# Out units that change PSUM banks behind a pair of scores instead of at a TensorE drain

## Chip, cores and metric

The kernel runs on one NeuronCore of a Trainium2 chip. The metric is the device time of one execution in microseconds (us); lower is better. TensorE (PE) has a loader for weights (PEld) beside its matmuls; VectorE is DVE, ScalarE is ACT, GpSimd is POOL, SyncE is SP.

## What is computed

With x of 2048 tokens by 576 channels in fp32:

```
g = sigmoid((x * gate_w).sum(-1))
q, k, v = split(x @ wqkv), 32 heads of 18
a = concat(softmax(q k^T / sqrt(18)) v) @ wo
h = gelu(layernorm(x) @ w1 + b1)            # 576 -> 4608
b = h @ w2 + b2                             # 4608 -> 576
out = g * a + (1 - g) * b
```

## The kernel before

Matmul operands that need it are split into a high and a low part, and a product is the sum of three matmuls (high x high, high x low, low x high). A first stage projects q, k and v, normalizes x and writes the pieces to scratch in device memory. Then one long loop does attention and the MLP together, and the output projection follows at its end.

**The loop** runs over 32 attention units (two heads and half of the queries each) and 16 steps of 128 keys in each, 512 steps. A step does two sets. A set is `s2`, a pair of score matmuls of the second pass (L247; two row groups of TensorE, one head each) whose two results ScalarE turns into exponentials (L250), and `next_round`, a pair of score matmuls of the first pass (L206) for a later unit whose row maxima VectorE takes (L208). The scores go round a ring of five PSUM banks, `score_bank`; a set uses four of them. On even steps the products of exponentials with V (`pv`, L265) stand behind the first set of the step.

**The MLP fills in.** `mlp` is a generator that issues one pair of matmuls at a time and says where a piece ends (`cut`). `fill` takes one piece (`atom`) behind a set: none behind the first set of an even step, where `pv` stands, one behind the second (`piece[0]` = 0), one behind each set of an odd step (`piece[0]` = 1 and 2). So four sets and three pieces make a round of two steps.

There are two kinds of MLP work. `h_pair` makes two chunks of 128 hidden channels for 512 tokens: 27 pairs of matmuls with 512 columns (L443) into two banks of the pool `ps_w`, then the gelu on ScalarE (L464, L496, L494) and GpSimd, handed out by `defer` (so many slots later) and `queue_end` (when the planner's clock `now` has passed the end that it reckons for GpSimd's queue). `out_pair`, an *out unit*, multiplies four chunks for 128 tokens with w2: 24 pairs of matmuls with 288 columns (L523), again into two banks of `ps_w`, which VectorE adds to the accumulator (L532). A group of four chunks takes one `h_pair`, then the four out units of the group before, then the other `h_pair`; there are 36 groups and 144 out units.

In an out unit, row group 0 holds one half of the hidden channels and row group 1 the other. In the first turn, 12 pairs, row group h adds into bank h; in the second turn, 12 pairs, into bank 1 - h. Two row groups may not write one bank at a time, so the first turn has to be through before the second begins. The kernel before has a drain on TensorE's queue at that place (L512).

The pieces of a unit that begins behind the second set of an even step are 7, 8 and 9 pairs (`ends = {7, 15}`), so the drain stands inside the middle piece, behind five of its eight pairs.

Of the kernel before, what the change touches and what calls it, by code (L numbers as in the profile page):

```python
# [8 lines left out]
F32 = mybir.dt.float32  # L9
F32R = mybir.dt.float32r  # L10
AF = mybir.ActivationFunctionType
# [16 lines left out]
G = 4  # L28
NFC = F // P
NG = NFC // G  # L30
ND = 288
# [26 lines left out]
def gated_mix_kernel(ctx: ExitStack, tc: tile.TileContext, x, wqkv, wo, w1, b1, w2, b2, gate_w, out):  # L58
    nc = tc.nc
# [3 lines left out]
    const = ctx.enter_context(tc.tile_pool(name="const", bufs=1))  # L63
# [14 lines left out]
    ident = const.tile([P, P], F32, name="ident")  # L78
# [19 lines left out]
    def psum(pool):  # L98
        return pool.tile([P, TB], F32, name="ps")
# [27 lines left out]
    def defer(n, fn):  # L127
        later.append((slot[0] + n, fn))
# [189 lines left out]
    def mlp():  # L318
# [65 lines left out]
        def ready(table, key):  # L384
            while key not in table:
                bg.pop(0)[1]()
            return table[key]
# [23 lines left out]
                          lambda c: load_w2(c + 2))  # L411

        open_pairs = [0]

        def cuts(n, pieces):

            return {(k * n + pieces - 1) // pieces for k in range(1, pieces)}
# [83 lines left out]
        def out_pair(i, t, acc):  # L501

            tb, g = seq[i]
            tok = slice(t * P, (t + 1) * P)
            cs = [slice(nn * ND, (nn + 1) * ND) for nn in range(2)]
            ps = [psum(ps_w) for _ in range(2)]
            ends = {7, 15} if piece[0] == 0 else cuts(24, (3, 2, 1)[piece[0]])
            k = 0
            for turn in range(2):
                if turn == 1:  # L510

                    nc.tensor.drain()  # L512
                for j in ORDER:
                    while (i, j) not in HT:
                        cut[0] = 3
                        yield 0
                    hh, hl = HT[i, j]
                    w_ = ready(W2, (i * (G // 2) + j // 2, j % 2))
                    for h_, p_ in ((hh, 0), (hh, 1), (hl, 0)):
                        for h in (0, 1) if turn == 0 else (1, 0):  # L520
                            r = slice(64 * h, 64 * h + 64)
                            nn = h ^ turn
                            nc.tensor.matmul(ps[nn][:, :ND], h_[r, tok], w_[p_][r, cs[nn]],  # L523
                                             start=(k == 0), stop=(k == 6 * G - 1))
                        k += 1
                        if k < 6 * G:
                            if k in ends:
                                cut[0] = 1
                            yield 131
            for nn in range(2):  # L530
                dst = acc[:, t, cs[nn]]
                nc.vector.scalar_tensor_tensor(dst, ps[nn][:, :ND], 0.5, b2b[:, cs[nn]] if g == 0 else dst,  # L532
                                               op0=ALU.mult, op1=ALU.add)
            if g == NG - 1:
                tt = tb * 4 + t
                nc.gpsimd.tensor_scalar(acc[:, t, :], acc[:, t, :], gate1[:, tt:tt + 1], 1.0, op0=ALU.mult, op1=ALU.mult)

                def store():
                    nc.sync.dma_start(b_scr[tt * P:(tt + 1) * P, :], acc[:, t, :])
                    kept[0] += 1  # L540
                defer(12 if tb < NB - 1 else 4, store)
            cut[0] = 2
            yield 131
# [7 lines left out]
        def outs(i, between=()):  # L551

            tb, g = seq[i]
            if g == 0:
                ACC[tb] = x_tile().rearrange("p (t d) -> p t d", t=4)[:, :, :D]
            for t in range(4):
                if t == 2:
                    yield from between
                yield from out_pair(i, t, ACC[tb])
            for j in range(G):  # L560
                HT.pop((i, j))
                W2.pop((i * (G // 2) + j // 2, j % 2))
# [22 lines left out]
        for i in range(n + 1):  # L585
# [10 lines left out]
            if i < n and not inside:  # L596
                yield from pair(q + 1, held)

    stream = [mlp()]
    spent = [0.0]  # L600
    cut = [0]
    piece = [0]
# [31 lines left out]
    with ExitStack() as a:  # L634
# [172 lines left out]
        for tb in range(NB):  # L807
            work = [(qk_group, (tb, mt)) for mt in (range(9) if tb < 2 else (4, 0, 1, 2, 3, 5, 6, 7, 8))] + [(v_group, (tb, t, n)) for t in range(4) for n in range(2)]
            for g, (fn, args) in enumerate(work):
# [22 lines left out]
                if tb == NB - 1:  # L832
# [16 lines left out]
                    if g == 7:  # L849
                        ps = psum(ps_s1)  # L850
# [283 lines left out]
```

## Time and profile before

| | us |
|---|---|
| median of 3 runs | 2382.97 (2378.87 to 2385.91) |
| the profiled execution | 2379.91 |
| its span, first to last instruction | 2378.1 |
| TensorE matmuls, busy | 2308.8 (97%) |
| VectorE, busy | 1655.4 (70%) |
| ScalarE, busy | 1425.9 (60%) |
| mean granted TensorE clock | 0.987 |

A line of the timeline gives start, length, engine (PEld is the weight load), source line, operation, what is written from what, shape, and how many instructions it merges; in square brackets the idle time of the engine ahead of it and what ended it. In a source line's answer, "issue" is idle time that ended without any other engine's release. Ends of matmuls are modelled, starts are recorded, so the distances below are taken between starts.

### The profile page before, as it was taken

What the parts mean: (1) busy time and instruction counts of PE and PEld (TensorE: products, weight loads), DVE (VectorE), ACT (ScalarE), POOL (GpSimd) and SP (SyncE); (2) the same over time, 40 slices, a digit from 0 to 9 for tenths busy, and PEclk for the clock granted to TensorE, in tenths of its full rate; (3) what the DMA queues carried; (4) which work ended last, traced back from release to release, by engine and by line L of the source; (5) the groups of instructions that cost most, each with busy time, mean ns of one, the idle gap of its engine ahead of it and who ended that gap; (6) DMA issues with size and microseconds to landing.
All of it is one profiled execution on the core that took longest, in us unless ns stands there. A gap on an engine that the chain in (4) does not pass through costs nothing.

```text
span 2378.1 us, 51603 instructions
## 1 busy us (share of the span) xinstructions
PE 2308.8 (97%) x20585; PEld 1571.9 (66%) x20585; DVE 1655.4 (70%) x2890; ACT 1425.9 (60%) x2628; POOL 968.3 (41%) x964
## 2 busy tenths in 40 slices
PE   8999899999999999999999999999999999999889
PEld 7876566666666666666666666666656666666558
DVE  5467577777776777777777777777767777777424
ACT  4222367777676666666666666666656666666552
POOL 3001366666664433333454444433343334444500
PEclk9999899999999999999999999999999999999899
DMA  7748744545455423342354424232545343331254
GB/s 229 243 166 235 211 146 137 166 129 151 134 185 163 156 94 116 104 140 97 98 153 161 130 85 131 94 116 94 142 137 166 112 119 114 92 115 66 96 181 157
DMA packets 164874, 330.31 MB, mean 139 GB/s; under 512 B 57898, under 2 KB 84558, under 8 KB 153906
## 3 DMA queue, kind: packets, MB, share of 16 engines
q1 hardware_dynamic: 163050, 323.78, 43.4%
q8 instruction: 162, 2.65, 0.5%
q10 hardware_dynamic: 1584, 3.24, 0.4%
q14 instruction: 78, 0.64, 0.1%
HBM read 234.16 MB, written 96.58 MB: 139 GB/s over the span
## 4 chain that ended last, share of the span: by engine, by line
PE 89%; DMA 5%; DVE 3%; SPq 1%; issue 1%; ACT 0%; POOL 0%; DVEq 0%; ACTq 0%
PE ps L523 20%; PE ps L265 19%; PE ps L443 18%; PE ps L247 12%; PE ps L206 11%; PE ps L755 4%; PE ps L1030 2%; PE ps L776 2%; DVE m L208 1%; DMA big<-y_scr 1%; DMA x<-in_B_w_dram 1%; DMA v_scr<-vt 0%; PE ps L682 0%; SPq L121 0%; SPq L372 0%
## 5 line engine op out<-in xcount | busy, mean ns | idle before, releaser
L208 DVE TENSOR_REDUCE m<-ps 128x1 f32<-128x512 f32 x2048 | 1316.7, 685 | 478.5 <-PE ps L206 460.1
L250 ACT ACTIVATE p<-ps 128x512 f32<-128x512 f32 x1368 | 742.9, 596 | 435.9 <-PE ps L247 425.6
L162 POOL TENSOR_SCALAR zz<-zz 128x512 f32<-128x512 f32 x288 | 179.4, 623 | 843.6 <-ACT zz L496 828.6
L443 PE MATMUL ps<-big,w 64*128 64x512 f32 x3888 | 513.9, 394 | 0.1
L523 PE MATMUL ps<-w,hh 64*128 64x288 f32 x4352 | 491.2, 300 | 19.3 <-DMA w<-w_scr 7.1
L250 ACT ACTIVATE ring<-ps 128x512 f32<-128x512 f32 x680 | 369.4, 596 | 213.3 <-PE ps L247 206.5
L206 PE MATMUL ps<-ka,qa 54*128 54x512 f32 x2048 | 457.0, 416 | 14.3 <-DVE m L208 7.9
L247 PE MATMUL ps<-qa,ka 56*128 56x512 f32 x2048 | 455.3, 425 | 10.9 <-ACT p L250 5.3
L523 PEld LDWEIGHTS ps<-w,hh 64*128 64x128 f32 x4352 | 383.6, 186 | 76.2 <-issue 45.2
L443 PEld LDWEIGHTS ps<-big,w 64*128 64x128 f32 x3888 | 380.1, 186 | 76.9 <-ACT z L464 0.4
L162 POOL TENSOR_TENSOR zz<-zz,z 128x512 f32<-128x512 f32 x288 | 372.5, 1294 | 24.0
L247 PEld LDWEIGHTS ps<-qa,ka 56*128 56x128 f32 x2048 | 205.5, 185 | 227.8 <-DVE m L208 176.6
L265 PE MATMUL ps<-p,vt 128*32 128x512 f32 x2736 | 348.7, 604 | 2.7 <-DMA vt<-v_scr 2.7
L523 PE MATMUL ps<-w,hl 64*128 64x288 f32 x2176 | 334.6, 292 | 0.0
L206 PEld LDWEIGHTS ps<-ka,qa 54*128 54x128 f32 x2048 | 213.5, 187 | 87.8 <-ACT p L250 24.1
L162 POOL TENSOR_TENSOR w<-x,w 128x576 fp32r<-128x576 f32 (+1 forms) x54 | 98.5, 1837 | 317.2 <-DMA y_scr<-hh 169.1
L523 PEld LDWEIGHTS ps<-w,hl 64*128 64x128 f32 x2176 | 218.5, 185 | 4.9
L162 POOL TENSOR_TENSOR hl<-zz,hh 128x512 fp32r<-128x512 f32 x136 | 176.6, 1299 | 11.3
L265 PE MATMUL ps<-ring,vt 128*32 128x512 f32 x1360 | 180.5, 603 | 0.0
L265 PEld LDWEIGHTS ps<-p,vt 128*32 128x32 f32 x2736 | 72.0, 109 | 164.1 <-issue 153.7
L532 DVE SCALAR_TENSOR_TENSOR x<-ps,x 128x288 f32<-128x288 f32 x256 | 104.1, 449 | 23.7 <-PE ps L523 23.7
L755 PE MATMUL ps<-big,wqk 128*128 128x512 f32 x432 | 111.7, 408 | 2.9 <-ACT wqk L676 2.3
(98 smaller groups left out, 1374.4 us busy)
## 6 DMA issues: line engine op xcount, KB each, us to landing
w<-w_scr SPq DMA_DIRECT2D x54, 1152.0 KB
w<-w_scr SPq DMA_DIRECT2D x108, 576.0 KB
x<-in_B_w_dram SPq DMA_DIRECT2D x72, 288.0 KB
w_scr<-w SPq DMA_DIRECT2D x18, 1152.0 KB
w_scr<-w SPq DMA_DIRECT2D x36, 576.0 KB
big<-y_scr SPq DMA_DIRECT2D x42, 384.0 KB
qa<-qk_scr SPq DMA_DIRECT2D x192, 72.0 KB
ka<-qk_scr SPq DMA_DIRECT2D x84, 144.0 KB
```

The lines of the kernel that those rows point to most:

```text
L162: fn(*args, **kw)
L206: nc.tensor.matmul(ps, qa[r0:r0 + 54, t * P:(t + 1) * P], ka[r0:r0 + 54, kb * TB:(kb + 1) * TB], start=True, stop=True)
L208: nc.vector.tensor_reduce(M4[u][:, h, t, kb:kb + 1], ps, axis=AX.X, op=ALU.max)
L247: nc.tensor.matmul(ps[h], ka[r0:r0 + 56, kc * P:(kc + 1) * P], qa[r0:r0 + 56, qb * TB:(qb + 1) * TB], start=True, stop=True)
L250: nc.scalar.activation(RING[n % 3][:, qb, h], ps[h], AF.Exp, scale=SCALE)
L265: nc.tensor.matmul(OB[u][r:r + 32, :], v[:, k, 19 * h:19 * h + 32], RING[c % 3][:, qb, h, :], start=(k == 0), stop=(k == NT - 1))
L443: nc.tensor.matmul(ps[h], wt[w_][r, c, :], Y[s_][r, c, :], start=(k == 0), stop=(k == 26))
L523: nc.tensor.matmul(ps[nn][:, :ND], h_[r, tok], w_[p_][r, cs[nn]], start=(k == 0), stop=(k == 6 * G - 1))
L532: nc.vector.scalar_tensor_tensor(dst, ps[nn][:, :ND], 0.5, b2b[:, cs[nn]] if g == 0 else dst, op0=ALU.mult, op1=ALU.add)
L755: nc.tensor.matmul(ps, w_[:, c, ms], big[:, s_, :], start=(k == 0), stop=False)
L776: nc.tensor.matmul(ps[:, :ND], big[:, s_, tok], w_[:, c, cs], start=(k == 0), stop=False)
L1030: nc.tensor.matmul(ps[:, :ND], OT[b][2][:, s_, tok], w_part(w_, c)[:, cs], start=(k == 0), stop=(k == 13))
```

## The change

The drain is taken out. The first turn's last two matmuls now release a tiny activation on ScalarE, which copies one element of the identity into a one-element tile (`token`), and the second turn's first two matmuls wait for that activation. The edge of the first piece moves to the change of banks, so that a set of scores stands between the two turns: a unit that begins behind the second set of an even step has pieces of 12, 6 and 6 pairs; one that begins in another place has two pieces of 12 (before, two of 12 or one of 24). ScalarE's queue has the token ahead of the exponentials of the set that follows. The reserve for GpSimd's DMA descriptors in SBUF is set to 1024 bytes.

```diff
         open_pairs = [0]
+        token = const.tile([1, 1], F32, name="token")
+
+        def behind_of(later_, earlier):
+
+            tc.add_manual_dep(later_.ins, earlier.ins.name, mybir.DependencyInfo(
+                mybir.DependencyClass.Sync, mybir.DependencyReason.DATA), reason="row halves change banks")
...
-            ends = {7, 15} if piece[0] == 0 else cuts(24, (3, 2, 1)[piece[0]])
+            ends = {12, 18} if piece[0] == 0 else {12}
             k = 0
+            ends_at, seen = [], []
             for turn in range(2):
-                if turn == 1:
-
-                    nc.tensor.drain()
                 for j in ORDER:
...
-                            nc.tensor.matmul(ps[nn][:, :ND], h_[r, tok], w_[p_][r, cs[nn]],
-                                             start=(k == 0), stop=(k == 6 * G - 1))
+                            mm = nc.tensor.matmul(ps[nn][:, :ND], h_[r, tok], w_[p_][r, cs[nn]],
+                                                  start=(k == 0), stop=(k == 6 * G - 1))
+                            if k == 3 * G - 1:
+                                ends_at.append(mm)
+                            elif k == 3 * G:
+                                behind_of(mm, seen[0])
                         k += 1
+                        if k == 3 * G:
+
+                            seen.append(nc.scalar.activation(token, ident[:1, :1], AF.Copy))
+                            for mm in ends_at:
+                                behind_of(seen[0], mm)
                         if k < 6 * G:
                             if k in ends:
                                 cut[0] = 1
...
-    nc = _bacc.Bacc("TRN2", target_bir_lowering=False, num_devices=1)
+    nc = _bacc.Bacc("TRN2", target_bir_lowering=False, num_devices=1, dynamic_dma_scratch_size=1024)
```

## The prediction

> **What bounds the kernel now.** The page comes first: the engines' busy shares, then the chain that ended last. After it come the answers for the drain's line and for the out matmuls' line, then the timeline of single units.
>
> ```profile
> span 2378.1 us, 51603 instructions
> PE 2308.8 (97%) x20585; PEld 1571.9 (66%) x20585; DVE 1655.4 (70%) x2890; ACT 1425.9 (60%) x2628; POOL 968.3 (41%) x964
> ...
> PE 89%; DMA 5%; DVE 3%; SPq 1%; issue 1%; ACT 0%; POOL 0%; DVEq 0%; ACTq 0%
> ...
> L512 PEldq DRAIN  x144: 912/1132/2100, 307.6 to 2270.7; - x144
> ...
>   issue: 47.8, 145
> ```
>
> TensorE carries 89% of the last chain, so what lengthens or shortens its queue moves the end. There are 144 drains, one in each out unit, and before the out matmuls' weight loads TensorE's loader sat idle 145 times, 47.8 us in all, for nothing that another engine did ("issue"): that is the drains. The mean engine shares don't say what happens if they go; for that I read one unit. Call its four sets (a pair of second-pass scores, L247, then a pair of first-pass scores, L206) A, B, C, D; the products with V stand behind A, the unit's pieces behind B, C and D.
>
> ```profile
> 1001.10 0.41 PE L247 MATMUL ps<-qa,ka 56*128 56x512 f32 x2
> ...
> 1003.53 0.51 PE L247 MATMUL ps<-qa,ka 56*128 56x512 f32 x2
> ...
> 1004.10 0.44 PE L523 MATMUL ps<-w,hh 64*128 64x288 f32 x4
> 1004.12 1.09 ACT L250 ACTIVATE ring<-ps 128x512 f32<-128x512 f32 x2 [1.44 <-PE ps L247]
> ...
> 1005.03 0.40 PE L247 MATMUL ps<-qa,ka 56*128 56x512 f32 x2
> 1005.26 0.19 PEld L206 LDWEIGHTS ps<-ka,qa 54*128 54x128 f32 x2 [0.16 <-ACT ring L250]
> ...
> 1005.52 1.09 ACT L250 ACTIVATE p<-ps 128x512 f32<-128x512 f32 x2 [0.30 <-PE ps L247]
> 1005.60 0.30 PE L523 MATMUL ps<-w,hh 64*128 64x288 f32 x2
> ...
> 1006.13 0.30 PE L523 MATMUL ps<-w,hl 64*128 64x288 f32 x2
> 1006.50 0.30 PEld L523 LDWEIGHTS ps<-w,hh 64*128 64x128 f32 x4 [0.31 <-issue]
> 1006.51 0.53 PE L523 MATMUL ps<-w,hh 64*128 64x288 f32 x4
> ...
> 1006.88 0.30 PE L523 MATMUL ps<-w,hl 64*128 64x288 f32 x2
> ...
> 1007.01 0.41 PE L247 MATMUL ps<-qa,ka 56*128 56x512 f32 x2
> ...
> 1007.24 0.41 PE L206 MATMUL ps<-ka,qa 54*128 54x512 f32 x2
> ...
> 1007.48 0.44 PE L523 MATMUL ps<-w,hh 64*128 64x288 f32 x4
> 1007.51 1.09 ACT L250 ACTIVATE p<-ps 128x512 f32<-128x512 f32 x2 [0.91 <-PE ps L247]
> ...
> 1008.54 0.30 PE L523 MATMUL ps<-w,hl 64*128 64x288 f32 x2
> ...
> 1008.67 0.41 PE L247 MATMUL ps<-qa,ka 56*128 56x512 f32 x2
> 1008.89 0.81 DVE L532 SCALAR_TENSOR_TENSOR x<-ps,x 128x288 f32<-128x288 f32 x2
> ```
>
> A to B takes 2.43, B to C 1.50, C to D 1.98, D to the next A 1.66: 7.57 us. A pair of out matmuls costs (1008.54 - 1007.48)/8 = 0.1325. Two things stretch it. Around the drain (1006.13 to 1006.88) three pair steps take 0.75 instead of 0.40: 0.35 lost. And at C the weights of the first-pass scores wait for ScalarE's second exponential of B: five score banks, four taken by each set, so the third matmul of a set needs the bank that the previous set's second exponential frees.
>
> **The price of that second wait** decides here, since shorter pieces bring it nearer. Two more places show it:
>
> ```profile
> 1021.86 1.09 ACT L250 ACTIVATE p<-ps 128x512 f32<-128x512 f32 x2
> ...
> 1022.83 0.40 PE L247 MATMUL ps<-qa,ka 56*128 56x512 f32 x2
> 1023.00 0.19 PEld L206 LDWEIGHTS ps<-ka,qa 54*128 54x128 f32 x2 [0.21 <-ACT p L250]
> ...
> 1023.34 1.32 PE L443 MATMUL ps<-big,w 64*128 64x512 f32 x10
> ```
>
> ```profile
> 977.53 1.09 ACT L250 ACTIVATE p<-ps 128x512 f32<-128x512 f32 x2 [0.58 <-PE ps L247]
> ...
> 978.45 0.40 PE L247 MATMUL ps<-qa,ka 56*128 56x512 f32 x2
> 978.66 0.19 PEld L206 LDWEIGHTS ps<-ka,qa 54*128 54x128 f32 x2 [0.26 <-ACT p L250]
> ...
> 980.95 0.50 PE L247 MATMUL ps<-qa,ka 56*128 56x512 f32 x2
> ...
> 982.45 0.40 PE L247 MATMUL ps<-qa,ka 56*128 56x512 f32 x2
> ...
> 983.86 0.63 ACT L494 ACTIVATE zz<-zz 128x512 f32<-128x512 f32 x1
> ```
>
> Call lag the time from a set's start to the end of the previous set's exponentials. With no lag the work behind a set starts 0.47 after it (1007.01 to 1007.48). In the first fence the lag is 1022.95 - 1022.83 = 0.12 and the work starts at 0.51: 0.04 lost. At C above the lag is 1005.21 - 1005.03 = 0.18 and it starts at 0.57: 0.10 lost. In the second fence, at an A, the lag is 0.17 and A to B takes 2.50 instead of 2.43: 0.07 lost. So a lag above 0.08 to 0.10 is lost one for one.
>
> **The change, part by part.** *The drain goes:* 0.35 off each unit, 144 x 0.35 = 50 us. That alone would give 2330.
>
> *Twelve pairs behind B:* B to C becomes 0.57 + 12 x 0.1325 = 2.16. The lag at C, 0.18, turns into -0.48, and the 0.10 lost there comes back.
>
> *The wait by ScalarE* isn't in this trace; its stages are bounded by rows:
>
> ```profile
> L731 ACT ACTIVATE sd<-var x4: 206/207/208, 43.0 to 192.6; 128x4 f32<-128x4 f32 x4
> ...
> L225 ACT ACTIVATE mr<-ps x32: 251/268/268, 242.7 to 2237.9; 32x128 fp32r<-32x128 f32 x32
> ```
>
> From a score pair's start to its exponential's is 0.50 (1007.01 to 1007.51); a pair with 288 columns is 0.10 shorter than one with 512 (0.1325 against 0.23), so the token starts 0.40 after the twelfth pair, which is 0.27 after C starts. I take 0.21 for it, as for the 128x4 row, the nearest in size. A release reaches TensorE's loader 0.05 after ScalarE ends (1005.21 to 1005.26). The thirteenth pair's weights therefore load at C + 0.525, and since nothing was loaded ahead the fourteenth pair follows 0.24 later, as after the drain (1006.51 to 1006.88 less one step): C + 0.765. Unhindered, behind C's two pairs of scores, it would start at C + 0.60. The wait costs x = 0.165. Bounds: 0.35 from pair to reader, as VectorE shows at the unit's end (1008.54 to 1008.89), gives x = 0.115; the 0.268 of the small copy out of the banks gives x = 0.225. I keep 0.165. Queued behind the token on ScalarE are C's exponentials; they start at C + 0.50, the token ends at C + 0.475, so they are just covered. Without that cover each 0.1 of delay there is lost a second time. B's own exponentials end 0.7 before the token can start and aren't touched.
>
> The Trainium skill ("ScalarE: Activation LUTs", What ACT_TABLE_LOAD costs) gives an ACTIVATE with immediate scale and bias 186 ns plus 0.833 ns a column, which makes 187 ns for the token as an estimate. The nearest row here has 207; by the Trainium skill x would be 0.145 and the total 3 us lower.
>
> *Six pairs behind C and six behind D:* C to D is 0.765 + 5 x 0.1325 = 1.43. C's exponentials end at C + 0.50 + 1.09 = 1.59, so the lag at D is 0.16, and 0.08 is lost. D to A is 0.47 + 0.08 + 6 x 0.1325 = 1.345. D's exponentials end 1.59 after D, a lag of 0.245 at A: 0.155 lost, A to B 2.585. Before, the lag at D and A was below 0.1 (1.59 - 1.98, 1.59 - 1.66), so these two losses are new. Between C and A, x cancels: what the token delays D, the exponentials no longer do; it returns as lag at A. The unit is 7.355 + x.
>
> *The sum:* 2.585 + 2.16 + 1.43 + 1.345 = 7.52 against 7.57 for the unit shown. The others of its group are a little shorter; from 978.45 (the first A) to 1008.67 the four take 30.22. The first of them has its lag of 0.17 at A already, 0.07 that stays, and a tanh behind C's exponentials (983.86 to 984.49) that would end 0.11 after D's exponentials are due (982.45 + 1.43 + 0.50); I add half of that, 0.05. After: 4 x 7.52 + 0.12 = 30.20. That is 0.02 gained in each of 36 groups, under 1 us.
>
> *The rest* is small. A piece of twelve moves the planner's clock by 12 x 131 = 1572 ns instead of GAP's 1130, so steps of the gelu and of the weight splits are handed out earlier by that clock; worked through for the first unit of a group, the tanh still lands between C's and D's exponentials. A weight copy handed out just behind the token would start 0.3 later (0.475 instead of 0.18 after C); with one such in each of the nine groups of the first quarter that is 3 us against the change. Where the planner is late, a first pair and two units take 5 + 2 + 2 pieces instead of 5 + 1 + 3, the same. The smaller DMA scratch moves no time: all transfers are issued by SP, the last ones by ScalarE.
>
> So 50 us of drains come back as 24 for the token (144 x 0.165), 34 for the lags at D and A (144 x 0.235) and 3 for copies, less some 9 for the lag at C that ends (0.04 to 0.10 a unit): about 2 us slower in these terms, and the same by the group's 1 us less 3. That is no change. The profiled execution took 2379.91 (its span 2378.1 and 1.8 around it); the median of the runs shown is 2382.97, 3 us above. I write 2380, the profiled one's own.
>
> **The rivals.** *Faster: the thirteenth pair's weights don't wait.* If only the matmul waits and its weights are already loaded under C's scores, the pair starts at C + 0.535 and the next one step later, x = 0.07: 0.095 less a unit, 14 us, 2366. The same side is reached by shorter latencies: x = 0.115 gives 7 us, 2373, and a wait fully covered 24 us, 2356. Against the first speaks the row at 1005.26: the loader itself stands until ScalarE's release, and the next pair is late by it. For the second: x adds up latencies that were each read from another kind of instruction. The Trainium skill ("TensorE: Matmul & The Clock Gate", Part 3, The mechanism) has weight loads pulled ahead of matmuls in flight when their row groups don't conflict. By that rule this rival would hold; the load at 1005.26, which lacked a release, was not pulled ahead.
>
> *Slower: the token holds up C's exponentials.* If it ends later than C + 0.50 it delays them by as much, and through them D's first-pass scores and the lag at A. The token's end decides: if it takes the 0.268 of the small copy it ends at 0.535, the exponentials slide 0.035 and x is 0.225, 0.095 worse a unit, 14 us, 2394; if it also starts 0.05 later, both grow by that, 0.195 a unit, 28 us, 2408. For it: the cover is 0.025 thin, and every unit has it. Against it: ScalarE is idle at that place (0.30 before C's exponentials) and 60% busy in all.
>
> *The change doesn't do what it says:* if the 0.31 before the thirteenth pair is the bank swap's own and not the drain's, it stays and the lags come on top, some 2420. Against it: the loader waits there for nothing, and the drain is all that stands between.
>
> **How the numbers follow.** A measurement of this kernel can tell about 0.3%, 7 us, from no change. No change (x from 0.115 to 0.21, cover holds): 0.36, with 2373 to 2387 as its own range. Faster by more (x below that, or lags shorter than read): 0.31. Slower by more: 0.33, of which 0.02 for the last rival. The range reaches into both sides, 2362 to 2400, with about 2 in 10 outside.
>
> **What would show it.** In the profile after, the drain's line is gone and the "issue" idle before out weights near nothing; in its place the loader waits 0.1 to 0.2 for the token, some 140 times. B to C is 2.16, C to D 1.43, D to A 1.34, A to B 2.58; the idle time before L206's weights at D and at A is put down to L250. Units of 7.4 or less, or first-pass weights that don't wait at D, would show me wrong on the lags; exponentials that start more than 0.52 after C's scores would show the token in their way.

## The result and the profile after

The changed kernel takes 2384.86 us (median of 12 runs, 2380.78 to 2388.82); the kernel before, run beside it, 2385.86 (12 runs, 2378.64 to 2389.73). The ratio is 1.000, with a 95% interval of 0.9991 to 1.0009: no difference. The forecast was no change at 2380.0; the 5 us between come from the profiled execution of the kernel before (2379.91), from which the forecast was made: it lies 6 us under the median of the 12 runs. The profiled execution after took 2387.25.

The page after, first the span and engines, then the chain that ended last:

```profile
span 2385.4 us, 51516 instructions
PE 2320.7 (97%) x20585; PEld 1564.5 (66%) x20585; DVE 1654.6 (69%) x2890; ACT 1441.1 (60%) x2772; POOL 966.9 (41%) x964
...
PE 89%; DMA 5%; DVE 3%; SPq 1%; ACT 1%; issue 1%; POOL 0%; DVEq 0%; ACTq 0%
```

ScalarE has 144 instructions more, and TensorE still carries 89% of the chain. The token's own row, and what the out matmuls' line (now L527) sat idle for (us, times):

```profile
L536 ACT ACTIVATE token<-ident x144: 185/202/204, 309.8 to 2278.3; 1x1 f32<-1x1 f32 x144
```

```profile
  ACT token L536: 43.6, 141
...
  issue: 2.1, 1
```

The drain's 47.8 us of idle time without a releaser became 43.6 us of waiting for the token: 0.31 each time, in the place of 0.33. The exponentials (L250) are now what first-pass weights wait for more often. The waits of the loader, in us, times and the longest, before:

```profile
PEld ps L206 <- ACT p L250: 24.1, 112, 0.4
...
PEld ps L206 <- ACT ring L250: 11.0, 51, 0.3
```

and after:

```profile
PEld ps L206 <- ACT p L250: 41.4, 178, 0.3
...
PEld ps L206 <- ACT ring L250: 20.9, 88, 0.3
```

From 35.1 us in 163 waits to 62.3 in 266: the new lags at D and above all at A. One unit of the timeline after, from its A at 1002.25 to the next A:

```profile
1002.25 0.40 PE L247 MATMUL ps<-qa,ka 56*128 56x512 f32 x2
...
1004.82 0.50 PE L247 MATMUL ps<-qa,ka 56*128 56x512 f32 x2
...
1006.85 0.30 PE L527 MATMUL ps<-w,hl 64*128 64x288 f32 x2
1006.86 0.20 PEld L247 LDWEIGHTS ps<-qa,ka 56*128 56x128 f32 x2
1006.99 0.41 PE L247 MATMUL ps<-qa,ka 56*128 56x512 f32 x2
...
1007.25 0.20 ACT L536 ACTIVATE token<-ident 1x1 f32<-1x1 f32 x1 [0.76 <-PE ps L527]
1007.41 1.09 ACT L250 ACTIVATE p<-ps 128x512 f32<-128x512 f32 x2
1007.50 0.30 PEld L527 LDWEIGHTS ps<-w,hh 64*128 64x128 f32 x4 [0.32 <-ACT token L536]
...
1008.41 0.39 PE L247 MATMUL ps<-qa,ka 56*128 56x512 f32 x2
...
1008.84 1.09 ACT L250 ACTIVATE p<-ps 128x512 f32<-128x512 f32 x2 [0.33 <-PE ps L247]
...
1009.69 0.40 PE L247 MATMUL ps<-qa,ka 56*128 56x512 f32 x2
1009.98 0.19 PEld L206 LDWEIGHTS ps<-ka,qa 54*128 54x128 f32 x2 [0.22 <-ACT p L250]
```

A to B takes 2.57, B to C 2.17, C to D 1.42, D to A 1.28: 7.44. The token starts 0.40 after the twelfth pair (1006.85 to 1007.25), and the loader stands until it is through. Behind it C's exponentials start 0.42 after C's scores, not 0.50 (the reason stands with e7 below).

To compare whole executions I cut the loop into rounds, from one A to the next, and matched them by number with a later execution of the kernel before (e5 below). The median change of each kind of round, times its count, is called *regular*; what single rounds take beyond that, *excess*. After: regular -10.9 us, excess +14.3. So the units did become shorter, and something else took it back. Both sums are rough, since they hang on which rounds are counted as one kind: sorted by work and place in the group alone, the changed kernel has -8 and +13, and with the place in the attention unit as well, -1 and +6. Medians of units and single rounds don't hang on it.

### The profile page after: what moved, and what is told of

It reads as the page before. It is cut to its first block, busy times and chain, and to the rows that moved or that the text cites. A ratio compares the mean times of both kernels' runs of the same rounds, so it can differ in the third digit from the quotient of the medians.

```text
span 2385.4 us, 51516 instructions
## 1 busy us (share of the span) xinstructions
PE 2320.7 (97%) x20585; PEld 1564.5 (66%) x20585; DVE 1654.6 (69%) x2890; ACT 1441.1 (60%) x2772; POOL 966.9 (41%) x964
## 4 chain that ended last, share of the span: by engine, by line
PE 89%; DMA 5%; DVE 3%; SPq 1%; ACT 1%; issue 1%; POOL 0%; DVEq 0%; ACTq 0%
PE ps L527 19%; PE ps L265 19%; PE ps L449 18%; PE ps L247 12%; PE ps L206 12%; PE ps L768 3%; PE ps L1043 2%; PE ps L789 2%; DVE m L208 1%; DMA x<-in_B_w_dram 1%; DMA qk_scr<-hh 1%; DMA dn<-oe 1%; PE ps L695 1%; DMA v_scr<-vt 0%; DMA bt<-b_scr 0%
## 5 line engine op out<-in xcount | busy, mean ns | idle before, releaser
L250 ACT ACTIVATE p<-ps 128x512 f32<-128x512 f32 x1368 | 742.6, 597 | 333.4 <-PE ps L247 318.9
L206 PE MATMUL ps<-ka,qa 54*128 54x512 f32 x2048 | 472.4, 426 | 15.0 <-DVE m L208 8.8
L527 PE MATMUL ps<-w,hh 64*128 64x288 f32 x4352 | 467.9, 300 | 8.3 <-DMA w<-w_scr 6.8
L250 ACT ACTIVATE ring<-ps 128x512 f32<-128x512 f32 x680 | 369.3, 597 | 166.2 <-PE ps L247 164.3
L527 PEld LDWEIGHTS ps<-w,hh 64*128 64x128 f32 x4352 | 370.3, 186 | 70.5 <-ACT token L536 43.3
L527 PE MATMUL ps<-w,hl 64*128 64x288 f32 x2176 | 332.5, 293 | 0.0
L527 PEld LDWEIGHTS ps<-w,hl 64*128 64x128 f32 x2176 | 216.4, 185 | 0.0
L162 POOL TENSOR_TENSOR hl<-zz,hh 128x512 fp32r<-128x512 f32 x136 | 176.8, 1300 | 11.4
```

What stands on the lines that cost most here:

```text
L162: fn(*args, **kw)
L206: nc.tensor.matmul(ps, qa[r0:r0 + 54, t * P:(t + 1) * P], ka[r0:r0 + 54, kb * TB:(kb + 1) * TB], start=True, stop=True)
L250: nc.scalar.activation(RING[n % 3][:, qb, h], ps[h], AF.Exp, scale=SCALE)
L527: mm = nc.tensor.matmul(ps[nn][:, :ND], h_[r, tok], w_[p_][r, cs[nn]], start=(k == 0), stop=(k == 6 * G - 1))
```

## Experiments

The befores beside the runs had medians of 2385.91 (e1 to e4), 2384.40 (e5 to e8) and 2384.55 (e9 to e11).

### The parts by themselves: drain or token, old pieces or new

**e2_drain12** is the kernel before, drain kept, with the new edges alone.

```diff
-            ends = {7, 15} if piece[0] == 0 else cuts(24, (3, 2, 1)[piece[0]])
+            ends = {12, 18} if piece[0] == 0 else {12}
```

> The kernel before with the drain, only its pieces are 12, 6 and 6, so that the drain stands behind a set of scores (one part of the change alone). By the prediction's terms C to D is 1.265 + 0.345 = 1.61, D to A 1.265 with no lag at D, the lag at A is 0.32 and costs 0.23: a unit of 7.67, 0.10 more than before, 14 us slower. If instead a drain behind scores costs less than in mid-piece (only what is left of the last matmul), C to D would be 1.40 and the kernel as fast as the changed one or faster; that would mean the way by ScalarE brings nothing over the drain.

It took 2421.80, a ratio of 1.0147 (1.0133 to 1.0161): 36 us slower. The loader's waits, and the drain's place in the timeline:

```profile
PEld ps L523 <- issue: 82.6, 145, 2.3
```

```profile
1011.97 0.41 PE L247 MATMUL ps<-qa,ka 56*128 56x512 f32 x2
...
1012.73 0.30 PEld L523 LDWEIGHTS ps<-w,hh 64*128 64x128 f32 x4 [0.55 <-issue]
```

Behind scores the drain leaves the loader idle 0.57 each time (82.6/145), against 0.33 in the middle of a piece, and the unit grows by the lag at A besides (0.33; there is none at D). About 14 us had been expected, with the drain priced as in the middle of a piece; the third and fourth units of a group take 7.76, where 7.67 was expected. Some 7 of the 36 us are one round at 548 us, the stall described under the planner's clock. The new edges alone are a loss.

**e3_token789** is the changed kernel with the old edges: the token in the middle of a piece, with no scores behind it.

```diff
-            ends = {12, 18} if piece[0] == 0 else {12}
+            ends = {7, 15} if piece[0] == 0 else cuts(24, (3, 2, 1)[piece[0]])
```

> The changed kernel with the old pieces 7, 8 and 9, so that the wait by ScalarE stands in mid-piece with no scores behind it (the other part alone). The token is queued behind C's exponentials, which end at C + 1.55; the twelfth pair starts at C + 1.1. So the token ends at about C + 1.7, and three pair steps from the twelfth on take 0.90 instead of 0.75: 0.15 to 0.25 more than with the drain in each unit, 20 to 36 us slower than before (0.9 to 1.5%). If the scores between the turns hide nothing, it would be no slower than the changed kernel.

2424.87, ratio 1.0157 (1.0141 to 1.0173): 39 us slower, a little beyond the 20 to 36 expected.

```profile
PEld ps L527 <- ACT token L536: 89.3, 144, 2.8
```

0.62 a time, nearly twice the drain's 0.33. So the change is two losses that make up for each other: the token needs the scores as its cover, and the edges that give the cover bring the lags.

### Which engine carries the token

**e4_vector** lets VectorE copy the element.

```diff
-                            seen.append(nc.scalar.activation(token, ident[:1, :1], AF.Copy))
+                            seen.append(nc.vector.tensor_copy(token, ident[:1, :1]))
```

> The changed kernel with the token on VectorE (a copy of one element) instead of ScalarE. In the changed kernel C's exponentials start 0.42 after C's scores, against 0.50 before and 0.50 predicted. Theory C: the token on ScalarE makes the exponential behind it start sooner, since ScalarE isn't idle ahead of it. Then with the token on VectorE they start at 0.49 again, the idle time of first-pass weights at D grows by about 0.07, while the token itself comes back 0.05 to 0.1 sooner (VectorE reads a finished pair at 0.35, and its small copies take 0.17): no change in all within 0.3%. Rival: the early start has another cause (place in the unit); then the exponentials still start at 0.42 and the kernel is 7 to 14 us faster than the changed one.

2379.05 (11 runs), ratio 0.9972 (0.9963 to 0.9981): 6.9 us faster, just inside the 0.3% that had been expected as no change. A unit's B, C and D and the A behind them:

```profile
1005.58 0.41 PE L247 MATMUL ps<-qa,ka 56*128 56x512 f32 x2
...
1005.78 0.14 DVE L536 COPY token<-ident 1x1 f32<-1x1 f32 x1 [0.31 <-PE ps L527]
...
1005.98 0.30 PEld L527 LDWEIGHTS ps<-w,hh 64*128 64x128 f32 x4 [0.20 <-DVE token L536]
...
1006.07 1.09 ACT L250 ACTIVATE p<-ps 128x512 f32<-128x512 f32 x2 [0.97 <-PE ps L247]
...
1006.87 0.41 PE L247 MATMUL ps<-qa,ka 56*128 56x512 f32 x2
...
1007.21 0.19 PEld L206 LDWEIGHTS ps<-ka,qa 54*128 54x128 f32 x2 [0.27 <-ACT p L250]
...
1008.34 0.40 PE L247 MATMUL ps<-qa,ka 56*128 56x512 f32 x2
```

The first row is C, 1006.87 is D, 1008.34 the next A. The token starts 0.34 after the twelfth pair (median) and takes 0.142, and the loader goes on at C + 0.40 instead of 0.51. C to D is 1.30 in the median (1.41 with ScalarE). But C's exponentials now start 0.49 after C, as before the change, and 0.43 with the token on ScalarE (medians of the units). These 0.06 come back as lag at D. Written with E for the time from a set's scores to the end of its exponentials and x for what the token's wait costs, the unit is 5.765 + E + x (the prediction's 7.355 less its E of 1.59): 5.765 + 1.52 + 0.163 = 7.45 with ScalarE (7.447 in medians), 5.765 + 1.58 + 0.045 = 7.39 with VectorE (7.393).

**e7_vector_wake** gives both: VectorE carries the token, and an activation that nobody waits for stands ahead of C's exponentials on ScalarE.

```diff
+        token2 = const.tile([1, 1], F32, name="token2")
...
-                            seen.append(nc.scalar.activation(token, ident[:1, :1], AF.Copy))
+                            seen.append(nc.vector.tensor_copy(token, ident[:1, :1]))
                             for mm in ends_at:
                                 behind_of(seen[0], mm)
+                            wake = nc.scalar.activation(token2, ident[:1, :1], AF.Copy)
+                            for mm in ends_at:
+                                behind_of(wake, mm)
```

> The wait goes round by VectorE, and a second tiny copy on ScalarE stands where the token stood, waiting for the same matmuls, with nothing waiting for it. With the token on VectorE the wait cost 0.045 instead of 0.16, but C's exponentials started at 0.49 instead of 0.43. Theory C: ScalarE starts an exponential 0.06 sooner when it has just run something. Then here C's exponentials start at 0.43, C to D stays 1.30, the lag at D is 0.21 instead of 0.27, a unit takes 7.33 instead of 7.39: 8 us faster than the kernel with the token on VectorE alone, 15 us faster than before (0.6%). Rival: the second copy costs ScalarE or TensorE as much as it brings, no difference.

The exponentials start at C + 0.43 again, and the third and fourth units of a group take 7.33 (7.39 in e4). So an activation ahead of them is enough. The theory for it, that ScalarE starts sooner when it has just run something, is not what the traces show. In e3 the token stands behind C's exponentials, and D's come after nearly 1 us of idle time:

```profile
1016.49 0.40 PE L247 MATMUL ps<-qa,ka 56*128 56x512 f32 x2
...
1016.92 1.09 ACT L250 ACTIVATE p<-ps 128x512 f32<-128x512 f32 x2 [0.99 <-PE ps L247]
```

They start at 0.43 all the same. What differs is a wait. Some exponentials wait for their scores and for an earlier instruction of ScalarE itself; ahead of these the trace has one more instruction on ScalarE's queue, an EVENT_SEMAPHORE (a bare wait for a counter). In e4, of the C's after 0.98 of idle time, 88 have it and start at 0.49, and 49 lack it and start at 0.43. The kernel before has both too: its C's, after 0.31 of idle time, start at 0.48 with it (82) and at 0.43 without (50). An activation that stands ahead has made that wait already. The row in the changed kernel, in e4 and in e7:

```profile
L250 ACTq EVENT_SEMAPHORE  x422: 17/17/38, 255.9 to 2334.9; - x141
```

```profile
L250 ACTq EVENT_SEMAPHORE  x613: 17/17/38, 257.0 to 2326.9; - x154
```

```profile
L250 ACTq EVENT_SEMAPHORE  x418: 17/17/38, 256.4 to 2325.3; - x140
```

The regular sum of e7 is -22.8 us, 5 better than e4's -17.6. But the time is 2378.08 (12 runs), ratio 0.9977 (0.9966 to 0.9988), no better than e4; about 15 us were expected. The excess is +15.9 here. How much of the 5 us is left with another sorting of the rounds, and why it doesn't reach the end, stays open.

### The planner's clock

Where did the excess come from? The largest single round (+7.5 us) is an out unit at 546 us. Its timeline after:

```profile
545.35 0.50 PE L247 MATMUL ps<-qa,ka 56*128 56x512 f32 x2
...
547.51 0.40 PE L247 MATMUL ps<-qa,ka 56*128 56x512 f32 x1
551.36 1.16 ACT L367 ACTIVATE w<-x 128x1152 fp32r<-128x1152 f32 x1 [6.99 <-issue]
552.43 1.07 ACT L250 ACTIVATE ring<-ps 128x512 f32<-128x512 f32 x2
...
553.06 0.28 PEld L247 LDWEIGHTS ps<-qa,ka 56*128 56x128 f32 x1 [5.49 <-ACT ring L250]
```

B's scores are done at 545.85; their exponentials start at 552.43, because a weight copy (L367) stands ahead of them on ScalarE and waits for its load. The loads' line and who waited for it, after:

```profile
L346 SPq DMA_DIRECT2D x<-in_B_w_dram x36: 595/637/6328, 189.3 to 660.9; - x36
...
  ACT w L367: 16.8, 7
```

One issue of a load took 6.3 us on SP's queue, and copies waited for loads seven times. The edit that could do this is the piece of twelve: it moves the planner's clock by 12 x 131 = 1572 ns in the place of 1130, so loads and weight copies are handed out earlier. The load here and in the kernel before:

```profile
539.40 7.01 SPq L346 DMA_DIRECT2D x<-in_B_w_dram  x2
```

```profile
548.51 1.36 SPq L346 DMA_DIRECT2D x<-in_B_w_dram  x2
```

In the changed kernel it is issued 1.1 us behind the 13 loads of q, k and v pieces (533.59 to 538.30), in the kernel before 10 us behind them. That these loads hold up its issue is likely, not shown. **e1_clock** charges the new pieces as the old ones were charged and changes nothing else.

```diff
-                run_due(max(spent[0] - t, GAP))
+                ns = max(spent[0] - t, GAP)
+                if abs(ns - 12 * 131) < 1:
+                    ns = GAP
+                elif share == 2 and abs(spent[0] - t - 6 * 131) < 1:
+                    ns = 9 * 131
+                run_due(ns)
```

> The changed kernel, but the planner's clock is charged for out pieces as before (1130, 1130, 1179 ns instead of 1572, 1130, 1130), so that gelu steps and weight copies are handed out where the kernel before has them. Theory A: the units themselves have become shorter (0.33 us in a group of four and the round behind it, about 12 us in all) and the gain is lost again in the first quarter, where weight copies on ScalarE are handed out earlier and stand in front of exponentials (one waited 7 us). Then this kernel is 6 to 12 us faster than the kernel before (0.25 to 0.5%), and no weight copy starts with ScalarE idle in front of it for more than 0.5 us in the first quarter. Rival B: the long waits in that profile are variation between executions and the copies cost nothing; then it stays within 0.1% of the changed kernel, that is of the kernel before.

The stall is gone. The loads' line in e1:

```profile
L346 SPq DMA_DIRECT2D x<-in_B_w_dram x36: 595/639/1453, 189.6 to 666.2; - x36
...
  ACT w L367: 3.9, 1
```

The time is not better: 2385.07 (11 runs), ratio 0.9999 (0.9991 to 1.0008); the 6 to 12 us of theory A did not come. The excess fell from 14.3 to 8.0; 4.1 of what is left is new and lies in six fourth units of the first quarter, where the copy now stands right behind the token:

```profile
444.29 0.40 PE L247 MATMUL ps<-qa,ka 56*128 56x512 f32 x2
...
444.56 0.20 ACT L536 ACTIVATE token<-ident 1x1 f32<-1x1 f32 x1 [0.75 <-PE ps L527]
444.67 1.15 ACT L367 ACTIVATE w<-x 128x1152 fp32r<-128x1152 f32 x1
...
445.72 0.57 ACT L250 ACTIVATE p<-ps 128x512 f32<-128x512 f32 x1
```

C's exponentials start 1.43 after C there, a second late. With the token on VectorE that can't happen in this way, so the two edits together should be worth more than each: **e9_vector_clock** is e4's edit and e1's.

> The wait goes round by VectorE and the planner's clock is charged as before. In the profiles the units' gain is lost at three places: one stall of 7 us in the first quarter, which only the kernels with the new clock have (a weight copy on ScalarE, handed out before its load has landed, with exponentials behind it); 0.4 to 1 us at six first-quarter units with the old clock, where the copy now stands behind the token; and 0.3 us at some ten rounds where first-pass row maxima are finished. Here the first is gone by the clock and the second because no token stands on ScalarE. Theory A3 (these are the places): 0.50 us in 36 groups less 3 us, 13 to 15 us faster than before (0.55 to 0.65%), and 6 to 8 us faster than the token on VectorE with the new clock. Rival B3 (the stall is a matter of the profiled execution and of no weight in the others): no faster than with the new clock, 6 to 7 us (0.28%).

2373.20 (6 runs), ratio 0.9951 (0.9938 to 0.9964): 11.4 us faster than the kernel before, the fastest version here. Its regular sum is -17.1, its excess 5.7, and the six units have 0.15 in place of 4.1. Expected were 13 to 15 by the theory that the clock and the engine add up, 6 to 7 by the one that the clock is worth nothing; the interval, 8.6 to 14.8 us, leaves the second out. Not all of it need be the two edits: in the profiled execution 4.5 us against e5 lie in two rounds at 1728 us, where e5's TensorE waits and then has a granted clock of 0.62 to 0.70, and e9's has 1.00. e2 and e3, slower in all, gain 5.3 and 5.9 in the same two rounds, so these gains can't be put down to the edits. What VectorE's token costs, as the token's row and as waits of the out matmuls' line:

```profile
L536 DVE COPY token<-ident x144: 131/142/145, 314.3 to 2266.0; 1x1 f32<-1x1 f32 x144
```

```profile
  DVE token L536: 29.0, 141
```

**e10_after_again** (the changed kernel, unaltered) and **e11_clock_again** (e1, unaltered) ran beside it on one chip, to see whether the clock alone is worth a few us.

> The changed kernel once more, unchanged, on the same chip as the other two of this set. If the stall of 7 us belongs to the kernel, its profile has it again at the fifth set of the same attention unit (547 us), with the weight copy waiting for its load. Time: as before, within 0.1%.

> The changed kernel with the planner's clock charged as before, once more, now beside the changed kernel on one chip. By the profiles it has no 7 us stall, but loses about 5 us at six units whose weight copy stands behind the token: 2 to 6 us faster than the changed kernel by theory A3; no difference by B3, as the runs of the first set had it.

e10: 2385.73 (12 runs), ratio 1.0012 (1.0003 to 1.0021). e11: 2384.83 (12 runs), 0.9996 (0.9987 to 1.0005). By the ratios the clock is worth 3.8 us here; by the medians 0.9, and in the first set (after against e1) nothing. The traces say 14.3 and 12.6 of excess for the changed kernel, 8.0 and 11.7 with the clock held. A gain of 2 to 6 us isn't excluded, and it isn't shown. That the stall hangs on the clock is shown by the traces: after, e10, e4, e7 and e2, where the clock runs as in the change, each have one issue of an L346 load of over 5 us near 540 us and a round of +5.8 to +8.1 at that place; e1, e11, e9, e3 and the kernel before have none (their longest issue on that line is 1.55). A long issue alone is not the stall: every kernel, the one before too, has one of 5.7 to 8.1 us on the other load line (L352, 411 to 416 us) with no such round.

Another long round is in the changed kernel and in every run with a part of it: 13.05 to 15.31, where the two profiles of the kernel before have 11.05 and 11.72. In the changed kernel (15.31) it is at 745 us; VectorE stands 5.27 for a transfer there (3.42 in e5), and TensorE with it. It is there in e6 too (14.66), whose units up to that place are those of the kernel before, and in e2 (13.71), which keeps the old reserve for descriptors, so it needs neither the new units nor the smaller reserve; its cause stays open.

### Only the last three quarters

**e6_late** keeps the drain and the old edges in the first quarter of the tokens, where the weights are split and copied, and changes the other three.

```diff
+            new = tb > 0
             ends = {12, 18} if piece[0] == 0 else {12}
+            if not new:
+                ends = {7, 15} if piece[0] == 0 else cuts(24, (3, 2, 1)[piece[0]])
...
+                if turn == 1 and not new:
+                    nc.tensor.drain()
...
-                            elif k == 3 * G:
+                            elif k == 3 * G and new:
...
-                        if k == 3 * G:
+                        if k == 3 * G and new:
```

> The change in three quarters of the MLP only: the out units of the first 512 tokens keep drain and pieces 7, 8, 9; the others have token and 12, 6, 6. In the first quarter ScalarE and GpSimd also split the weights. Theory A2: the steady units give 0.32 us back in each group (27 groups left: 9 us) and the whole of it is lost in the first quarter, because weight copies get behind the token or in front of exponentials, whichever clock the planner has; then this kernel is 6 to 9 us faster than before (0.25 to 0.4%). Rival B2: the loss is spread over the run (irregular units, where the time is set by a transfer and a shorter unit gains nothing); then it is 0 to 2 us faster.

**e8_vector_late** is the same with the token on VectorE.

> The token on VectorE, in the last three quarters only. By the groups of its own trace the token on VectorE brings 0.50 us a group, 13.5 us in 27 groups; over all 36 groups it brought 6.9 us in all. Theory A2 (the first quarter loses what the rest gains): 11 to 13.5 us faster than before (0.5%). Rival B2 (loss spread): 5 to 6 us.

e6 took 2379.86 (12 runs), ratio 0.9988 (0.9978 to 0.9999); e8 2376.11 (12 runs), 0.9969 (0.9956 to 0.9983). No issue of an L346 load is long in either (at most 1.43 and 1.61). That is 0.2 to 5.2 and 4.1 to 10.5 us faster than the kernel before. The theory that the first quarter loses what the others gain asked for 6 to 9 and 11 to 13.5; both lie outside. The rival, a loss spread over the run, asked for 0 to 2 and 5 to 6, and both intervals reach into that.

The traces bear it out without any sorting of rounds. Against e5, the first 64 rounds of the loop take 6.4 us more in the changed kernel (the stall is in them), and the other 191 only 1.7 less; in e6 these 191 take 3.0 less, where 27 groups at 0.33 would make 9. So the first quarter takes something back, but most of what the units gain in the other three is lost there too. The smaller reserve for descriptors shows no cost of its own: e6's first 58 rounds, with the units of the kernel before, take 485.7 us, and e5's 485.6.

**e5_before_again** is one more look at the kernel before.

> The kernel before once more, unchanged, for a second profile: how far single executions differ stage by stage. If the first profile of before was an ordinary one, its stages agree within 1 us (253.6 up to the loop, 535.4 for the first eight attention units, 100.8 for the last 43 sets). If it was a quick one, the first stage takes 255 to 256 and the first eight units 537 to 540, and so much of the difference between the profiles of before and of the changed kernel is variation.

It took 2383.76, 4 us above the first profiled execution. The difference lies ahead of the loop (256.2 us against 253.6) and in its first eight attention units (536.7 against 535.4); the second and third eight agree within 0.1 (506.1 and 510.8). So regular sums can be compared to a fraction of a us, whole executions to some 4.

## Why the prediction was right

**Right by its steps.** Token start 0.40 behind the twelfth pair (forecast 0.40), its length 0.202 (0.21), release to loader 0.05 (0.05), x = 0.163 (0.165), B to C 2.16 (2.16), C to D 1.41 (1.43), A to B 2.58 (2.585), all in medians; the loader's waits at D and A are put down to L250, and the lost time came back in the terms named: token, lags, copies. The Trainium skill ("ScalarE: Activation LUTs", What ACT_TABLE_LOAD costs) made the token 187 ns; the row has 202, nearer to the 207 of the 128x4 row.

**Mis-sized, with opposite signs.** Two terms were wrong and nearly cancelled. *D to A: 1.29, not 1.345.* C's exponentials were put at C + 0.50, the start of those that make the extra wait; behind the token, which has made it, they start at 0.43, and so do D's. The trace of before has starts of both kinds, and the prediction read one. The lag at D is 0.10 instead of 0.16, and the unit 7.45 instead of 7.52. That makes some 0.33 us a group, 11 us in all by the regular sum, where the forecast had under 1. *The rest: some 14 us by the same sorting, not 3.* The piece of twelve and the planner's clock were named, and worked through for the first unit of one group with the result that the tanh lands well; the weight copies of the first quarter weren't. There the earlier copy meets a load that isn't there: 7.5 us in one round, 1.0 and 0.5 in two more. The round at 745 us adds 3.6 against e5. Some 3 us of the rest are gains that the rounds in which the first-pass maxima are finished don't pass on, 0.25 to 0.35 in each of ten. Not all of the rest is accounted for. Had only the first term been wrong, the kernel would have come out some 8 us faster by these sums (11 less the 3 of copies). So the steps inside a unit were right for their reasons; that the whole came out at no change is in part luck, since two errors of opposite sign met. Two criteria of the prediction were loose besides: the loader's wait for the token is 0.31, not 0.1 to 0.2 (only x of it is lost, since the loader would have been ahead by the rest), and "units of 7.4 or less" was met by the first units of a group (7.38) but not by the third and fourth (7.44).

**The rivals.** *Weights that don't wait* fell: the thirteenth pair's weights are what waits, 141 times. The Trainium skill's rule ("TensorE: Matmul & The Clock Gate", Part 3, The mechanism) of weight loads pulled ahead doesn't help where the load itself carries the wait. The other half of that rival, a wait that is nearly covered, became true with VectorE: x = 0.045. *The token holds up the exponentials* fell, and the reverse held: they start earlier. Only where a weight copy slips in between (e1), or waits ahead of them (the stall), are they late. *The idle time is the bank swap's own* fell: with the token gone through sooner the idle time is shorter (0.21 in e9, 29.0/141).

## What to carry to other kernels

A drain that is replaced by a wait round another engine costs what the round trip exceeds its cover: move the edge so that other work covers it, count what the moved edge costs in other waits, and choose the carrier by its latency, by what queues behind it and by which waits it takes off that (here VectorE, 0.142 long, rather than ScalarE, 0.202 long and ahead of the exponentials). When sizes of pieces change, look for a planner that is charged by them: it moves copies and loads in places far from the edit. And when a large change moves nothing, match the rounds of the two traces one by one: a regular gain and a few costly rounds look the same in the total as no effect. But sort the rounds in more than one way before believing the two sums.

## What was unexpected of the chip

An activation that waits for scores alone starts 0.43 us after them, and one that must also wait for an earlier instruction of its own engine 0.49, after 0.3 us of idle time as after 1 us; a useless activation ahead of it that makes the second wait wins the 0.06 back (e7). A drain behind a pair of 512-column scores leaves the loader idle 0.57, between 288-column pairs 0.33.

The stall at 546 us costs more than its idle time. In the changed kernel's windows (busy us of each engine, granted clock, DMA share, GB/s):

```profile
547.00:553.00 6.00, 0.91 (x13) 0.57 (x9) 0.41 (x1) 1.64 (x3) 0.85 (x2) 0.81 0.95 289
553.00:557.00 4.00, 3.94 (x25) 3.45 (x27) 1.62 (x3) 2.28 (x7) 2.25 (x1) 0.50 0.03 10
```

For 4 us after it TensorE's clock was granted at 0.50: some 2 us on top of the 5.5 of waiting, which is the round's 7.5.
